# A fused linear-attention and SiLU feed-forward kernel: first states from PSUM by VectorE, weight pieces in one row, a new order of tasks

## The chip, the cores and the metric

The kernel runs on one core of one Trainium2 chip. The metric is device time in microseconds (us) of one execution of the whole program. Lower is better.

## What is computed

The reference has two parts. The first is a gated linear recurrence over 768 steps, for each of 4 batches and 8 heads with head dimension 48:

```python
f = 1.0 / (1.0 + np.exp(-f_logit))
for t in range(S):
    state = f[:, :, t, :, None] * state + einsum('bhd,bhe->bhde', k[:, :, t], v[:, :, t])
    y[:, :, t] = einsum('bhd,bhde->bhe', q[:, :, t], state)
```

The second part takes the rows `y` as a 3072 x 384 matrix `x` (batch and step as rows, head and dimension as columns) and gives `silu(x @ w_in) @ w_out`, with `w_in` 384 x 2048 and `w_out` 2048 x 384. Inputs and output are float32.

## The kernel before, in words

**Tiling.** Each batch's 768 steps are cut into 6 chunks of 128. Two chunks make a pair; there are 12 pairs P. Pairs 0 to 3 (form "T") hold chunks 0 and 1 of one batch and interleave even and odd steps, so each DMA row is 384 bytes. Pairs 4 to 11 (form "N") hold the same chunk of two batches, with rows of 192 bytes.

**The stages of a pair,** with the name that each has as a task (`P` pair, `i` one of its two chunks):

- `f`, `k`, `q`, `v`: input loads, issued on SP's queue (line 239). A whole pair's tensor is 128 x 768 float32, listed as 384 KB; `k.4.0` and `k.4.1` are halves.
- `E` (line 246) and `L` (lines 258, 261): ScalarE exp and log, which give the log of the gate. `cs` (lines 322 to 332): TensorE sums it along the steps by a triangular matrix. `ia` and `a` (line 334): ScalarE exp of plus and minus that sum. `al` (lines 276, 336): the decay over the chunk.
- `ki` and `qg` (line 339): k times `ia` and q times `a`, on VectorE (letter V) or GpSimd (G). `vb` (line 341): v cast to bf16.
- `tq` (line 346) and `qkc` (line 185 or 187, called from 350 or 352): the transposition of k and q by TensorE and its copy out of PSUM, or `qkD` (line 354): the same by a DMA on SP's queue.
- `sc` (lines 363, 367): the products of q and k. `at` (line 371): VectorE masks them, two per chunk. `y` (lines 283, 379, 383): the output rows; `yi` is the part that comes from the earlier state, where it is issued apart.
- `d` (lines 295, 400): k times v, summed over the chunk, in PSUM. `sd` (lines 404, 406) adds the earlier state, or only copies `d` into SBUF for the first chunk of a batch. `su` (line 414) multiplies by the decay into the bf16 state `st`. It is two instructions, one for each half of the head pairs, of 48 partitions and 4 x 48 elements.
- `yc`, `yT`, `xc` (lines 387, 391, 393): y to bf16, transposed by TensorE, copied; or `yD` (line 395) by a DMA on SP's queue.
- `mi` (line 269): 8 tasks a pair, x @ w_in, each for 256 of the 2048 columns; pairs 0 and 1 have each in two halves, for one chunk each (`mi.0.3.1` is pair 0, task 3, chunk 1). `si` (line 274): ScalarE SiLU. `mo` (line 304): 4 tasks a chunk, the product with w_out. `oc` (line 307), `so` (lines 314, 316): out of PSUM, and stored.
- `wi` (line 216) and `wo` (line 219): the weights in 4 pieces each, cast from float32 to bf16 by DMAs that GpSimd issues. `wi.n` serves tasks `mi` 2n and 2n+1, `wo.n` the n-th `mo` of each chunk.
- `idle`: TensorE products of zeros into a free PSUM bank (line 459), `idle.512.5::2` being 5 of 512 columns into bank 2.

**What sets the order.** The text PLAN names every task with its engine letter (A ScalarE, V VectorE, G GpSimd, S SP, P TensorE) and, after the second colon, the buffers that it takes. Tasks are issued in that order (line 504), and each engine and queue works its own in the order given. A task waits for its data and for the former users of its buffer; one that waits holds back all that stand behind it on its engine. ScalarE loads a table (line 507) at each change between exp/log and SiLU. Ahead of the plan stand masks and memsets (lines 479 to 503).

In the plan before, POOL's queue (GpSimd) has `wi` and `wo` between other tasks: `su.0.0 wi.1 ki.2.1 wi.0 qg.2.0 qg.2.1 wi.2 su.1.0 wi.3 su.0.1 vb.2.1 wo.0 su.2.0 ki.3.0 wo.1 qg.3.0 wo.2 vb.3.1 su.2.1 vb.3.0 wo.3`. SP's queue begins `f.0.0 f.0.1 f.2.0 f.1.0 q.0.0 k.0.0 k.1.0 v.0.0 q.1.0 f.3.0 k.2.0 q.2.0 v.1.0 f.4.0 v.2.0 q.3.0 k.3.0`.

Of the kernel before, what the change touches and what calls it, by code (L numbers as in the profile page):

```python
# [53 lines left out]
mi.2.2:P:4 si.2.3:A:2 si.1.7:A: tq.3.1:P:7 v.4.0:S:5 si.2.0:A: mi.2.1:P:1 qkc.3.1:V:1 si.0.6:A: mo.0.1.0:P:6 si.2.1:A: vb.3.1:G:6 tq.3.0:P:3
su.2.1:G:0 si.1.6:A: mi.2.5:P:7 qkc.3.0:V: si.1.5:A: mi.2.7:P:2 vb.3.0:G:0 si.2.5:A: wo.3:G: mo.0.0.0:P:1 si.2.7:A: v.5.0:S:0 si.2.2:A: ki.4.1:G:3
d.3:P:5,0 sd.3.0:V:0 sc.3.0:P:3,7 sc.3.1:P:2,4 su.1.1:G:0 at.3.0.1:V:2 mo.0.0.1:P: at.3.1.0:V:3 E.5.0:A:0 mo.2.1.0:P:5 su.3.0:G:0 mo.1.1.0:P:7
L.5.0:A:2 f.6.0:S:2 mo.1.1.1:P: sd.3.1:V:1 at.3.1.1:V: mo.0.0.2:P: at.3.0.0:V: mo.2.1.1:P: y.3:P:2,0 mo.1.1.2:P: q.4.1:S:4 mi.2.6:P:4 mi.2.4:P:3
# [4 lines left out]
vb.5.1:A:2 mo.2.0.3:P: qkD.4.1:S:0 mi.3.1:P:7 oc.2.0:V:3 vb.4.0:V:3 mi.3.0:P:2 si.3.2:A:3 oc.2.1:V:4 si.3.3:A: qg.4.0:V: mo.1.0.2:P: si.3.5:A:
mi.3.6:P:0 q.6.0:S: ki.5.0:G:4 si.3.1:A: f.8.0:S:3 tq.4.0:P:3 si.3.0:A: so.1.1:G: mi.3.4:P:5 vb.4.1:A:4 qg.5.0:V: q.7.0:S:1 vb.6.1:A:5 qg.5.1:V:1
mo.1.0.3:P: si.3.4:A: ki.5.1:G: cs.6.1:P:1 qkc.4.0:A:1 mi.3.7:P:4 cs.6.0:P:7 si.3.7:A: d.4.0:P:2 qkD.5.0:S:2 mo.3.1.0:P:5 sd.4.0:V:0 si.3.6:A:
oc.1.0:V:5 vb.5.0:A:0 mo.3.1.1:P: sc.4.1:P:3,4 sc.4.0:P:2,0 at.4.1.0:V:0 mo.3.1.2:P: qkD.5.1:S:3 a.6.1:A:2 at.4.0.0:V:1 mo.3.0.0:P:6 E.8.0:A:0
# [4 lines left out]
mi.4.0:P:7 si.4.7:A: si.4.1:A: tq.6.0:P:4 si.4.0:A: y.5.0:P:0 k.8.1:S:1 mi.4.6:P:2 qkc.6.0:A:1 yc.5.0:V:1 k.7.0:S:2 mi.4.5:P:1 si.4.4:A: so.0.0:S:  # L70
y.5.1:P:7 si.4.2:A: mo.4.0.0:P:0 su.5.1:G:0 si.4.5:A: v.7.0:S:2 mo.4.1.0:P:4 yc.5.1:A:2 vb.8.1:A:6 su.4.1:G:0 sc.6.1:P:3,6 si.4.6:A: sc.6.0:P:1,7
q.7.1:S: at.6.1.0:V:0 mo.4.0.1:P: yD.5.0:S:0 at.6.0.0:V:1 cs.8.1:P:2 mo.4.1.1:P: at.6.1.1:V: E.7.0:A:1 at.6.0.1:V: cs.8.0:P:3 yT.5.1:P:1 mo.4.0.2:P:
sd.5.0:V:1 L.7.0:A:2 k.8.0:S: vb.7.0:G:3 y.6.1:P:6 v.10.0:S:3 su.5.0:G:0 a.8.1:A:0 y.6.0:P:7 ia.8.0:A:2 so.3.0:S: mo.4.1.2:P: ia.8.1:A:3 mo.4.0.3:P:
# [467 lines left out]
```

## Time and profile before

| | before |
|---|---|
| median of the runs | 182.53 us (182.09, 182.53, 183.05) |
| the profiled execution | 181.74 us |
| its span, first to last instruction | 179.9 us |
| TensorE busy | 170.3 us |
| ScalarE busy | 134.9 us |
| VectorE busy | 83.2 us |
| GpSimd busy | 59.9 us |
| mean granted TensorE clock | 0.991 |

The span is what the trace covers; the profiled execution's own time is 1.84 us longer, for what lies around the instructions. A timeline row gives start, duration, engine, line, operation, and `out<-in`; in square brackets stands the idle time of the engine just before, and what ended it. A row of the chain gives start, length, and the engine and line that the chain runs through. A row by stretches gives length, then busy time and count for TensorE matmul (PE), weight load, VectorE (DVE), ScalarE (ACT) and GpSimd (POOL), then granted clock, DMA share and GB/s. A row by groups gives count, total busy us, mean ns of one, then idle before. A DMA queue's row gives packets, MB and share of the time of 16 engines; q1 carries what SP issues, q0 what GpSimd issues.

### The profile page before, as it was taken

The page shows a single profiled execution, that of the slowest core. Times are in us where ns is not written, and L with a number is a line of the kernel's source. Part 1 is how long each engine was busy: PE and PEld are TensorE (multiplying, and loading weights), DVE is VectorE, ACT ScalarE, POOL GpSimd, SP SyncE. Part 2 cuts the span into 40 slices and gives each one's busy share as a digit, 9 for nine tenths or more (in the row PEclk, how much of TensorE's full clock was granted, in tenths as well). Part 3 has the DMA queues.
Part 4 walks back from the last instruction along what each step waited for, and adds up shares of the span by engine and source line. Part 5 has one row for each costly group of instructions (what it writes and reads, how often), then busy time and mean ns, then how long its engine had stood idle before and what let it go on. Part 6 is the DMA issues. An engine that isn't in the chain of part 4 may idle for free.

```text
span 179.9 us, 4982 instructions
## 1 busy us (share of the span) xinstructions
PE 170.3 (95%) x2039; PEld 130.0 (72%) x2040; DVE 83.2 (46%) x165; ACT 134.9 (75%) x252; POOL 59.9 (33%) x107
## 2 busy tenths in 40 slices
...
GB/s 142 315 321 309 202 242 256 230 209 193 180 176 182 203 201 134 210 204 207 158 106 221 178 202 205 125 218 170 216 156 122 213 127 26 109 26 131 0 154 112
DMA packets 109574, 31.91 MB, mean 177 GB/s; under 512 B 103536, under 2 KB 109088, under 8 KB 109552
## 3 DMA queue, kind: packets, MB, share of 16 engines
...
q8 instruction: 16, 0.26, 0.6%
...
HBM read 25.17 MB, written 4.72 MB: 166 GB/s over the span
## 4 chain that ended last, share of the span: by engine, by line
PE 84%; ACT 6%; DVE 3%; DMA 2%; issue 2%; POOL 0%; POOLq 0%; DVEq 0%
PE pb L304 33%; PE pb L269 33%; PE pb L459 3%; DMA xT<-yb 2%; ACT x L334 2%; PE pb L346 2%; PE pb L379 2%; PE pb L383 2%; PE pb L367 2%; DVE atm L371 2%; PE pb L329 2%; DVE qk L339 1%; PE pb L391 1%; PE pb L295 1%; PE pb L363 1%
## 5 line engine op out<-in xcount | busy, mean ns | idle before, releaser
L304 PE MATMUL pb<-w_out_sb,hT 128*128 128x384 bf16 (+1 forms) x416 | 70.7, 313 | 0.1
L269 PE MATMUL pb<-xT,w_in_sb 128*128 128x256 bf16 (+1 forms) x672 | 70.1, 257 | 0.7 <-DMA xT<-yb 0.5
L274 ACT ACTIVATE hT<-pb 128x512 bf16<-128x512 f32 x96 | 51.0, 611 | 23.2 <-PE pb L269 23.1
L269 PEld LDWEIGHTS <-w_in_sb 128*128 128x128 bf16 x672 | 56.9, 98 | 8.2 <-issue 0.9
L304 PEld LDWEIGHTS <-hT 128*128 128x128 bf16 x416 | 37.9, 97 | 18.1
L414 POOL TENSOR_TENSOR st<-sd,al 48x192 bf16<-48x192 f32 x40 | 20.6, 516 | 54.7 <-PE pb L379 18.2
L371 DVE TENSOR_TENSOR atm<-pb,triu 128x512 bf16<-128x512 f32 x32 | 20.0, 682 | 15.2 <-PE pb L367 15.2
L187 DVE COPY ob<-pb 128x384 f32<-128x384 f32 (+1 forms) x16 | 8.3, 526 | 36.0 <-PE pb L304 35.9
L334 ACT ACTIVATE x<-pb 128x384 f32<-128x384 f32 x48 | 22.0, 511 | 3.3 <-PE pb L329 1.5
L507 ACT ACT_TABLE_LOAD x17 | 21.8, 1283 | 0.3
L339 POOL TENSOR_TENSOR qk<-k,x 128x384 bf16<-128x384 f32 x11 | 11.4, 1038 | 14.9 <-DVE vb L187 13.5
L339 DVE TENSOR_TENSOR qk<-k,x 128x384 bf16<-128x384 f32 x13 | 11.9, 936 | 8.3 <-DMA k<-in_k_dram 5.4
L404 DVE TENSOR_TENSOR sd<-pb,st 128x384 f32<-128x384 f32 x16 | 8.6, 550 | 12.6 <-PE pb L400 6.1
L316 POOL DMA_DIRECT2D out_dram<-ob x7 | 4.0, 569 | 29.5 <-ACT ob L185 21.1
L339 DVE TENSOR_TENSOR qk<-q,x 128x384 bf16<-128x384 f32 x17 | 11.4, 688 | 3.3 <-DMA q<-in_q_dram 1.8
L246 ACT ACTIVATE e<-f 128x768 f32<-128x768 f32 (+1 forms) x13 | 10.5, 804 | 2.0 <-DMA f<-in_f_logit_dram 2.0
L185 ACT CAST yb<-pb 128x384 bf16<-128x384 f32 x16 | 7.6, 490 | 3.6 <-PE pb L383 2.4
L371 DVE TENSOR_TENSOR atm<-pb,mask 128x512 bf16<-128x512 f32 x16 | 10.1, 680 | 0.4 <-PE pb L363 0.4
L339 POOL TENSOR_TENSOR qk<-q,x 128x384 bf16<-128x384 f32 x7 | 7.1, 1019 | 7.4 <-ACT x L334 5.8
L459 PE MATMUL pb<-zero,triu 128*128 128x512 bf16 x19 | 7.1, 525 | 1.5 <-POOL triu masks.py:66 1.4
L185 ACT COPY ob<-pb 128x384 f32<-128x384 f32 (+1 forms) x10 | 4.4, 456 | 4.6 <-PE pb L304 4.6
L346 PE MATMUL pb<-ident,qk 128*128 128x128 bf16 x80 | 6.7, 234 | 0.4 <-DVE atm L371 0.4
...
## 6 DMA issues: line engine op xcount, KB each, us to landing
f<-in_f_logit_dram SPq DMA_DIRECT2D x11, 384.0 KB, 5.5
...
q<-in_q_dram SPq DMA_DIRECT2D x4, 384.0 KB, 5.2
k<-in_k_dram SPq DMA_DIRECT2D x4, 384.0 KB, 4.9
v<-in_v_dram SPq DMA_DIRECT2D x4, 384.0 KB, 7.3
w_in_sb<-in_moe_w_in_dram POOLq DMA_DIRECT2D x4, 384.0 KB, 7.5
```

Source lines behind the costliest of these rows:

```text
L185: nc.scalar.copy(dst, src)
L246: return nc.scalar.activation(e, at("f", P)[:, j * w:(j + 1) * w], AF.Exp, scale=-1.0)
L269: nc.tensor.matmul(h[:, i, cols], w_in_sb[:, kk, n * 128:(n + 1) * 128], at("xT", P)[:, kk, cols], start=(kk == 0), stop=(kk == KT - 1))
L274: return nc.scalar.activation(at("hT", P)[:, 2 * j:2 * j + 2, :], at("h", P, j).rearrange("p (n c) -> p n c", n=2), AF.Silu)
L304: nc.tensor.matmul(at("o", P, i)[:, cols], at("hT", P)[:, n, i * C:(i + 1) * C], w_out_sb[:, n, cols], start=(n == 0), stop=(n == NT - 1))
L334: nc.scalar.activation(at(kind, P, i).rearrange("p h d -> p (h d)"), at("cs", P, i)[:, 0:HD], AF.Exp, scale=1.0 if kind == "ia" else -1.0)
L339: ENG[eng].tensor_mul(at("qk", P, i)[:, j, :, 0:D], heads("qk"[j], P, i), at("ia" if j else "a", P, i))
L346: nc.tensor.transpose(t_ps[:, j, p, :], at("qk", P, i)[:, j, 2 * p:2 * p + 2, :], ident)
L371: ENG[eng].tensor_mul(at("atm", P, i)[:, r], at(f"s{r}", P, i).rearrange("p (n c) -> p n c", c=C), mask[:, None, :].to_broadcast([C, NP, C]))
L414: ENG[eng].tensor_mul(at("st", P, i)[lo:lo + D, :, r * D:(r + 1) * D], src[lo:lo + D, :, r * D:(r + 1) * D], al_of(P, i)[lo:lo + D, :, Non ...
L459: nc.tensor.matmul(buf["pb", int(got)][:, 0:rest[0]], triu, zero[:, 0:rest[0]], start=True, stop=True, skip_group_check=True)
L507: nc.scalar.preload_act_table_set(TABLES[mode])
```

## The change

Three things change.

1. `sd.0.0`, `sd.1.0`, `sd.2.0` (ScalarE) and `sd.3.0` (VectorE), the copies of a first chunk's `d` out of PSUM, are no longer in the plan. `su.0.0`, `su.1.0`, `su.2.0` and `su.3.0` move from GpSimd to VectorE and read `d` from PSUM (line 411).
2. POOL's queue begins `vb.1.1 ki.1.0 qg.1.1 wi.1 wi.2 wi.0 ki.2.0 qg.2.0 qg.2.1 wi.3 wo.0 wo.1 su.0.1 wo.2 wo.3 ki.3.0 su.1.1 ki.3.1`: all eight weight pieces stand behind the tasks of the pairs 0 and 1.
3. The whole PLAN is new: order, buffers, and the engine of some tasks (`oc` on ScalarE 10 to 15, `xc` 4 to 8, `yc` 16 to 12; `qg` on GpSimd 7 to 11; `so` on POOL's queue 12 to 15). The other tasks are the same, 10 `tq`, 14 `qkD`, 12 `yT` and 12 `yD` among them. The `idle` products are 24 instead of 20, all ahead of the first `mi`.

Two further edits in the code do nothing with this plan: the pair's halves are of one chunk, so `b, c` come out as before, and no pair of form T has a `qkD`.

```diff
-f.0.0:S:0 f.0.1:S: f.2.0:S:1 f.1.0:S:2 q.0.0:S:0 E.0.0:A:0 E.0.1:A: k.0.0:S:0 L.0.0:A:0 L.0.1:A: idle.512.11::0 cs.0.1:P:0 E.2.0:A:1 k.1.0:S:1
...
-idle.512.3::3 sc.0.0:P:3,7 al.2:A:1 ia.2.0:A:4 su.0.0:G:0 sc.0.1:P:5,1 f.4.0:S:0 at.0.0.1:V:0 E.3.0:A:0 at.0.0.0:V: tq.1.0:P:7 al.1:A:2 a.2.0:A:2
-wi.1:G: v.2.0:S:2 at.0.1.0:V:1 tq.1.1:P:2 L.3.0:A:0 qkc.1.1:V:1 qkc.1.0:A: ki.2.1:G:4 idle.512.1::3 cs.3.1:P:3 at.0.1.1:V: cs.3.0:P:4 a.3.1:A:1
-ki.2.0:V:0 wi.0:G: sc.1.0:P:5,2 ia.3.1:A:0 at.1.0.0:V:2 y.0:P:7,1 a.2.1:A:3 qg.2.0:G: al.3:A:3 yc.0.0:A:0 at.1.0.1:V: q.3.0:S:3 sc.1.1:P:6,3
-vb.1.1:A:2 yi.0.1:P: qg.2.1:G: at.1.1.1:V:3 yT.0.0:P:5 vb.1.0:A:3 tq.2.0:P:7 yc.0.1:A:1 at.1.1.0:V: d.1:P:2,3 a.3.0:A:4 wi.2:G: yT.0.1:P:1 sd.1.0:A:1
-tq.2.1:P:6 xc.0.1:V:0 ia.3.0:A:2 xc.0.0:V: su.1.0:G:0 k.3.0:S:3 y.1:P:2,1 qkc.2.0:A:0 sd.0.1:V:0 mi.0.3.0:P:4 yc.1.0:V:2 mi.0.3.1:P: wi.3:G:
...
+f.2.0:S:0 k.0.0:S:0 f.0.1:S:1 f.0.0:S: E.2.0:A:0 f.1.0:S:2 L.2.0:A:0 v.1.0:S:0 q.0.0:S:0 idle.512.11::0 cs.2.1:P:0 E.0.1:A:1 E.0.0:A: k.1.0:S:1
+cs.2.0:P:1 L.0.1:A:1 L.0.0:A: E.1.0:A:0 q.1.0:S:1 idle.512.1::2 cs.0.0:P:2 cs.0.1:P:3 a.0.0:A:0 vb.1.1:G:0 f.3.0:S:3 L.1.0:A:2 ia.0.1:A:1 cs.1.0:P:4
+a.0.1:A:2 qg.0.0:V:0 v.0.0:S:1 cs.1.1:P:5 ia.1.0:A:3 ki.0.1:V:1 al.1:A:0 ia.0.0:A:4 qg.0.1:V: al.0:A:1 ia.1.1:A:0 k.2.0:S:2 ki.0.0:V: vb.1.0:A:1
+idle.512.4::6 tq.0.1:P:6 ki.1.0:G:2 ia.2.0:A:1 tq.0.0:P:7 qkc.0.1:V:0 a.1.0:A:2 q.2.0:S:2 qkc.0.0:A: qg.1.0:V: ki.1.1:V:3 a.1.1:A:4 idle.512.3::2
+tq.1.0:P:2 q.3.0:S:3 a.2.0:A:3 qg.1.1:G: sc.0.0:P:3,4 qkc.1.0:A:1 sc.0.1:P:6,7 at.0.0.1:V:0 k.3.0:S:3 wi.1:G: at.0.0.0:V: E.3.0:A:1 idle.512.2::5
+tq.1.1:P:5 at.0.1.0:V:1 wi.2:G: d.1:P:1,4 qkc.1.1:A: v.2.0:S:2 su.1.0:V:0 wi.0:G: at.0.1.1:V: al.2:A:2 L.3.0:A:0 idle.512.3::2 sc.1.0:P:2,3 ki.2.0:G:4
+sc.1.1:P:6,1 at.1.0.1:V:2 vb.0.0:A:2 cs.3.1:P:5 vb.0.1:A:3 at.1.1.0:V:3 qg.2.0:G: al.3:A:3 ia.2.1:A:2 d.0:P:7,3 at.1.1.1:V: a.2.1:A:0 cs.3.0:P:6
+ia.3.1:A:4 su.0.0:V:0 qg.2.1:G:2 y.0:P:0,1 a.3.0:A:1 at.1.0.0:V: yc.0.0:A:0 yi.0.1:P: tq.2.0:P:7 a.3.1:A:3 wi.3:G: yc.0.1:V:1 ia.3.0:A:0 y.1:P:0,2
+wo.0:G: ki.2.1:V: yc.1.0:A:2 yT.0.0:P:5 sd.0.1:V:0 yi.1.1:P: yT.0.1:P:1 yc.1.1:A:0 tq.2.1:P:6 xc.0.0:V:0 wo.1:G: xc.0.1:A: qkc.2.0:V:0 v.3.0:S:3
+yT.1.0:P:0 yT.1.1:P:3 xc.1.0:A:1 mi.0.2.0:P:2 qkc.2.1:V: su.0.1:G:0 xc.1.1:A: mi.0.3.0:P:5 mi.1.3.0:P:1 sd.1.1:V:1 mi.1.3.1:P: qg.3.0:V:3 wo.2:G:
+mi.0.2.1:P: sc.2.1:P:7,0 si.1.3:A:0 wo.3:G: qg.3.1:V:0 sc.2.0:P:3,6 at.2.1.1:V:0 mi.1.5.1:P:4 mi.1.2.1:P:1 at.2.0.0:V:1 mi.1.2.0:P: at.2.0.1:V:
+mi.0.3.1:P: mi.1.4.1:P:0 at.2.1.0:V: mi.1.4.0:P: mi.0.5.0:P:3 si.1.4:A: mi.1.0.0:P:6 mi.1.1.1:P:7 mi.1.0.1:P: f.5.0:S:0 mi.1.5.0:P: si.1.0:A:
+mi.0.1.1:P:0 si.0.3:A:1 mi.0.1.0:P: mi.0.5.1:P: si.1.5:A: ki.3.0:G: mi.0.0.0:P:6 si.0.1:A: mi.0.6.0:P:5 mi.0.0.1:P: su.1.1:G:0 mi.0.7.1:P:4 si.0.0:A:
+mi.0.7.0:P: si.0.2:A: mi.0.6.1:P: ki.3.1:G: mi.1.1.0:P: si.0.6:A: mi.1.7.0:P:0 tq.3.0:P:6 mi.1.7.1:P: qkc.3.0:A:1 mi.0.4.0:P:2 tq.3.1:P:5 si.1.7:A:
+mi.0.4.1:P: f.4.0:S:1 mo.0.0.0:P:6 qkc.3.1:A: mo.0.1.0:P:0 si.1.1:A: mi.1.6.1:P:5 si.0.5:A: mi.1.6.0:P: si.1.2:A: mo.1.1.0:P:7 si.1.6:A: mo.0.1.1:P:
...
+mo.3.0.0:P:7 si.3.2:A: q.7.0:S:1 oc.2.1:A:5 at.4.1.1:V: cs.6.1:P:5 mo.3.0.1:P: si.3.6:A: y.4.1:P:2 d.5.1:P:0 v.6.0:S:2 yc.4.1:V:0 su.4.1:G:0
...
@@ -234,6 +234,8 @@
                 n = 2 // parts
                 w = n * HD
+                if n == 1:
+                    b, c = us[j][0] - j, us[j][1]
@@ -351,7 +353,11 @@
         elif kind == "qkD":
-            nc.sync.dma_start_transpose(out=at("qkT", P, i).rearrange("p j n c -> p (j n) c"), in_=at("qk", P, i).rearrange("p j h d -> p (j h d)"))
+            if T:
+                dst = at("qkT", P).rearrange("p j n g s c -> p (j n) g s c")[:, :, :, i]
+            else:
+                dst = at("qkT", P, i).rearrange("p j n c -> p (j n) c")
+            nc.sync.dma_start_transpose(out=dst, in_=at("qk", P, i).rearrange("p j h d -> p (j h d)"))
```

More of the change, by code (lines that the diff above doesn't have):

```diff
@@ L54 @@
[L54 to L57, printed above, removed]
@@ L62 @@
[L62 to L65, printed above, removed]
@@ L70 @@
[L70 to L73, printed above, removed]
@@ new lines @@
+mi.2.0:P:6 xc.3.1:V: su.2.1:G:0 mi.3.6:P:3 si.2.3:A:2 mi.3.1:P:4 qg.4.0:V: si.2.7:A: k.4.1:S: su.3.1:G:0 si.2.5:A: mi.3.7:P:5 si.3.1:A:3 f.6.0:S:2
+mi.2.6:P:7 vb.5.1:A:0 si.3.7:A: d.4.0:P:0 v.4.1:S: mi.2.1:P:4 sd.4.0:V:0 si.2.6:A: qg.4.1:V:2 tq.4.0:P:5 si.2.4:A: mi.3.2:P:0 si.2.1:A: k.7.0:S:1
+si.2.0:A: mi.3.0:P:7 ki.4.1:G: qkc.4.0:A:0 cs.5.1:P:1 mi.3.5:P:4 qkD.4.1:S:1 si.3.0:A: mo.2.1.0:P:6 si.2.2:A: si.3.5:A: sc.4.0:P:5,7 v.7.0:S:1
+at.4.0.1:V:0 mo.2.1.1:P: k.5.0:S: at.4.0.0:V: mi.3.4:P:2 q.6.0:S:0 cs.5.0:P:4 ia.5.1:A:4 mo.2.1.2:P: al.5.1:A:1 al.5.0:A:0 ia.5.0:A:1 ki.5.1:V:4
@@ new lines @@
+mo.2.0.0:P:7 E.6.0:A:0 vb.4.1:V:1 f.7.0:S:3 mo.2.0.1:P: vb.5.0:A:2 v.9.1:S:3 a.5.1:A:2 mo.2.0.2:P: L.6.0:A:0 qg.5.1:G: d.4.1:P:5 mo.2.0.3:P:
+sd.4.1:V:1 a.5.0:A:3 y.4.0:P:1 mi.3.3:P:5 yc.4.0:V:2 su.4.0:G:0 oc.2.0:V:4 mo.2.1.3:P: si.3.3:A: f.8.0:S:1 si.3.4:A: sc.4.1:P:4,1 at.4.1.0:V:1
+mo.3.0.0:P:7 si.3.2:A: q.7.0:S:1 oc.2.1:A:5 at.4.1.1:V: cs.6.1:P:5 mo.3.0.1:P: si.3.6:A: y.4.1:P:2 d.5.1:P:0 v.6.0:S:2 yc.4.1:V:0 su.4.1:G:0
+mo.3.0.2:P: ia.6.1:A:0 cs.6.0:P:4 k.6.0:S: yT.4.0:P:6 E.7.0:A:1 ki.5.0:V:0 so.2.0:G: mo.3.0.3:P: qg.5.0:V: qkD.5.1:S:2 mo.3.1.0:P:1 L.7.0:A:1
@@ new lines @@
+si.4.3:A: sc.5.0:P:3,1 k.8.0:S:2 ki.6.0:V: si.4.2:A: mo.4.1.0:P:6 at.5.0.0:V:3 si.4.5:A: q.7.1:S: yT.5.1:P:0 mo.4.0.0:P:7 at.5.0.1:V: mo.4.1.1:P:
+qg.6.1:V: al.7.1:A:5 y.5.0:P:2 qkD.6.1:S:0 a.7.1:A:0 cs.8.1:P:5 yc.5.0:A:2 tq.6.0:P:3 ia.7.1:A:3 d.6.0:P:1 qkc.6.0:V:1 vb.7.1:A:3 cs.8.0:P:2
+yD.5.0:S:1 mo.4.0.1:P: ia.8.0:A:1 ki.7.1:V:4 ia.8.1:A:2 sc.6.0:P:4,3 qg.7.1:V: al.8.0:A:1 a.8.0:A:4 mo.4.0.2:P: qkD.7.0:S:2 a.8.1:A:3 at.6.0.1:V:0
+xc.5.1:A: mo.4.1.2:P: qg.8.1:G:0 at.6.0.0:V: qkD.7.1:S:3 d.6.1:P:2 sd.6.0:V:1 mo.4.0.3:P: su.5.0:G:0 mo.4.1.3:P: d.7.0:P:3 oc.4.1:A:4 sd.6.1:V:0
@@ new lines @@
+mi.7.1:P:7 si.7.4:A: oc.5.1:A:0 y.8.1:P:3 k.9.1:S: si.7.6:A: mi.7.5:P:5 so.5.1:G: yc.8.1:V:1 si.7.1:A: vb.9.1:V:5 v.10.1:S:4 mi.7.0:P:4 su.6.0:G:0
+si.7.5:A: cs.9.1:P:2 si.7.0:A: sc.8.0:P:6,3 q.11.0:S:5 at.8.0.1:V:1 mi.7.7:P:7 at.8.0.0:V: mo.7.0.0:P:5 k.10.1:S: si.7.7:A: si.7.2:A: mo.7.1.0:P:4
+so.3.0:S: cs.9.0:P:3 y.8.0:P:6 mo.6.0.0:P:7 yD.8.1:S:0 a.9.1:A:0 mo.7.0.1:P: yc.8.0:A:2 qg.9.1:G:1 ia.9.1:A:3 mo.7.1.1:P: ia.9.0:A:1 yD.8.0:S:
+E.10.0:A:0 ki.9.1:G: mo.7.0.2:P: mo.7.0.3:P: al.9.0:A:4 a.9.0:A:2 ki.9.0:G:2 qkD.9.1:S:3 L.10.0:A:1 mo.6.0.1:P: qg.9.0:V: mo.6.1.1:P: qkD.9.0:S:2
@@ new lines @@
+mo.8.1.0:P:6 sd.9.0:V:1 yc.9.1:A:1 yD.9.0:S:1 a.10.1:A:3 d.9.1:P:3 E.11.0:A:1 mo.8.0.0:P:2 qg.10.1:G: yD.9.1:S: mo.8.1.1:P: L.11.0:A:2 su.9.0:G:0
+mo.8.0.1:P: a.10.0:A:1 qkD.10.1:S:1 cs.11.0:P:4 oc.6.0:A:0 mo.8.0.2:P: a.11.0:A:2 ia.11.0:A:4 cs.11.1:P:5 qg.11.0:V:3 mo.8.1.2:P: a.11.1:A:0
+sd.9.1:V:1 ia.11.1:A:3 mo.8.1.3:P: vb.11.1:V:3 qg.10.0:V: mi.9.4:P:0 ki.11.0:V: qkD.10.0:S:0 mi.9.0:P:7 vb.10.1:V:4 si.9.4:A:0 vb.10.0:V:1 mi.9.3:P:4
+ki.11.1:G:2 qkD.11.0:S:2 mi.9.6:P:3 si.9.3:A: qg.11.1:G: mi.9.2:P:5 si.9.6:A: si.9.0:A: mi.9.1:P:0 so.6.0:G: qkD.11.1:S:3 si.9.2:A: su.9.1:G:0
```

83 lines of the change are left out of this document (33 added, 50 removed).

## The prediction

> **What bounds the kernel now.** I read the page first, then the span cut at the first and behind the last product with the weights, then the chain of waits about the cut.
>
> ```profile
> span 179.9 us, 4982 instructions
> PE 170.3 (95%) x2039; PEld 130.0 (72%) x2040; DVE 83.2 (46%) x165; ACT 134.9 (75%) x252; POOL 59.9 (33%) x107
> PE 84%; ACT 6%; DVE 3%; DMA 2%; issue 2%; POOL 0%; POOLq 0%; DVEq 0%
> ```
>
> ```profile
> 0.00:25.17 25.17, 19.50 (x285) 12.33 (x287) 17.43 (x47) 19.55 (x41) 11.04 (x29) 0.93 1.06 259
> 25.17:176.77 151.60, 150.78 (x1760) 117.64 (x1754) 65.73 (x119) 115.09 (x212) 48.90 (x79) 1.00 0.84 166
> 176.77:179.90 3.13, 0.00 (x0) 0.00 (x0) 0.00 (x0) 0.31 (x1) 0.00 (x0) 1.00 0.26 84
> ```
>
> TensorE bounds it. Behind 25.17, where the first `mi` starts, it stands still for only 151.60 - 150.78 = 0.82 us until its last product. What another order can win there is under 1 us. The last 3.13 us are one copy and the last stores, the same in both orders. So the question is when the first `mi` starts, and whether the new order keeps the rest as full. What held that start?
>
> ```profile
> 17.94 1.69 DVE qk L339
> 19.63 1.18 issue
> 20.80 0.69 DVE atm L371
> ...
> 21.53 0.48 PE pb L391 x3
> ```
>
> ```profile
> 18.48 1.97 POOL L339 TENSOR_TENSOR qk<-q,x 128x384 bf16<-128x384 f32 x2
> 17.86 3.02 DVE L339 TENSOR_TENSOR qk<-k,x 128x384 bf16<-128x384 f32 x1
> 138.35 0.99 POOL L339 TENSOR_TENSOR qk<-q,x 128x384 bf16<-128x384 f32 x1
> 138.41 1.35 DVE L339 TENSOR_TENSOR qk<-k,x 128x384 bf16<-128x384 f32 x1
> ```
>
> ```profile
> 20.00:21.00 1.00, 0.00 (x0) 0.00 (x0) 1.00 (x2) 0.75 (x3) 1.00 (x2) 1.00 1.24 181
> 21.00:22.00 1.00, 0.47 (x5) 0.47 (x5) 1.00 (x2) 0.40 (x1) 0.17 (x1) 0.50 1.16 184
> 23.00:24.00 1.00, 1.00 (x21) 0.86 (x17) 0.27 (x1) 0.35 (x1) 0.00 (x0) 0.50 1.09 266
> 25.00:26.00 1.00, 1.00 (x36) 0.96 (x28) 0.90 (x3) 0.43 (x1) 1.00 (x2) 1.00 1.20 212
> ```
>
> `ki.2.0` on VectorE lasts 3.02 us, until 0.43 behind the two `qg` of GpSimd (20.45). The later pair of rows repeats it: GpSimd ends at 139.34, VectorE at 139.76. So a product of two SBUF operands on VectorE that meets one on GpSimd ends 0.42 behind it. Behind `ki.2.0` stand four `at`; TensorE's `yT.0.0` needs their bank, and TensorE does nothing from 20 or just before to 21.53. Then its clock is granted at 0.50 up to about 24.6: 3 us at half speed, 1.5 of them lost. In all the old start loses about 3 us here.
>
> **The change, part by part.** *First states.*
>
> ```profile
> L185 ACT COPY sd<-pb 128x384 f32<-128x384 f32 x3 | 1.5, 512 | 2.2 <-PE pb L295 2.2
> L414 POOL TENSOR_TENSOR st<-sd,al 48x192 bf16<-48x192 f32 x40 | 20.6, 516 | 54.7 <-PE pb L379 18.2 <-DVE sd L404 10.9 <-DVE qk L339 9.1
> L187 DVE COPY ob<-pb 128x192 f32<-128x192 f32 x2 | 0.7, 358 | 21.4 <-PE pb L304 21.4
> L187 DVE COPY sd<-pb 128x384 f32<-128x384 f32 x1 | 0.6, 557 | 1.8 <-ACT hT L274 1.8
> L497 DVE MEMSET st<- 128x192 uint32 x4 | 0.8, 218 | 0.0
> ```
>
> Removed: 3 x 0.512 on ScalarE, 0.557 on VectorE, 8 x 0.516 = 4.1 on GpSimd. Added: 8 VectorE products of 192 elements from PSUM. No row shows one; the bounds are 0.218 (192 elements written, none read) and 0.557 (384 from PSUM). I take 0.36, the row of 192 from PSUM: 2.9 us in all. On TensorE's path this is worth nothing: the chain above runs through no `sd` or `su`. In the new order `su.0.0` lies just ahead of `yi.0.1`; at 0.557 it costs up to 0.4. I take 0: VectorE is otherwise ahead of ScalarE there.
>
> *Loads.* Units of 0.393 MB:
>
> ```profile
> q1 hardware_dynamic: 2129, 0.80, 62.1%
> q1 hardware_dynamic: 4192, 1.58, 115.1%
> 5.85 0.84 ACT L246 ACTIVATE e<-f 128x768 f32<-128x768 f32 x1 [0.35 <-DMA f<-in_f_logit_dram]
> ```
>
> The queue's rows are 0 to 5 us and 5 to 10 us: 0.316 MB/us from 5 on. The first two units (0.79) were moved by 5.0, and the exp on the second (`f.2`), which waited for the load, started at 5.85: 0.85 from moved to usable. In the new order `f.0` is the third unit (1.18 MB): 5 + 0.38/0.316 + 0.85 = 7.05; before it was the first. `f.1` is usable at 8.3, `k.1` (seventh) at 12.0. That is the price of putting `f.2` and `k.0` ahead.
>
> *The start.* In the new order ScalarE sets it.
>
> ```profile
> 4.58 0.92 ACT L258 ACTIVATE lf<-e 128x384 bf16<-128x384 f32 x2
> 8.98 1.58 ACT L258 ACTIVATE lf<-e 128x768 bf16<-128x768 f32 x2
> 10.50 2.03 ACT L334 ACTIVATE x<-pb 128x384 f32<-128x384 f32 x5
> 13.13 1.09 ACT L185 COPY qkTT<-pb 128x1024 bf16<-128x1024 bf16 x1
> 19.32 0.96 ACT L185 CAST vb<-v 128x384 bf16<-128x384 f32 x2
> ```
>
> Ends overlap the next start by about 0.1 to 0.2, so the steps are 0.41, 0.75, 0.39, 0.89 and 0.42. From 7.05: `E.0.0` and two halves of `L` to 8.3, `E.1.0` to 9.05. Then, up to `yc.1.1`, which frees the bank of `mi.0.2.0`: 3 whole E or L (2.25), 16 `ia` or `a` (6.24), 4 `al` (0.4, an estimate), 3 `qkc` (2.67), 3 `vb` (1.26), 3 `yc` (1.2): 14.0, which is 23.05. One wait lies inside: `ki.1.0` on GpSimd starts at 12.25 (`k.1` at 12.0, behind a product of VectorE), ends at 13.25, so `ki.0.0` on VectorE ends at 13.7, `tq.0.0` at 14.2; ScalarE has come to `qkc.0.0` at 13.55. That adds 0.65: 23.7. Beside it `vb.0.1` ends at about 20.2, `d.0` takes 0.45, then VectorE's `su.0.0` 0.7 and `at.1.0.0` 0.6: 22.0; its `yc.0.1`, `ki.2.1`, `sd.0.1` (0.55, 0.55, 0.5) and `xc.0.0` (0.35) end at 23.9. With 0.1 or so at each of the last handovers I take the first `mi` at **24.4**; 23.9 would be none of them. `ki.2.0` and both `qg` of pair 2 are on GpSimd now, with `at` and `su` from PSUM on VectorE beside them, so the stall of 3.02 us has no place.
>
> What TensorE has done by then differs by three small tasks:
>
> ```profile
> 26.01 0.17 PE pb L379 x4
> 26.52 0.17 PE pb L391 x3
> ```
>
> `yi.1.1` and both `yT` of pair 1 lie ahead of the first `mi` now: 3 x 0.17 = 0.51 less behind it. The other work is the same; the four extra `idle` lie in gaps of the start.
>
> *The sum.* (24.4 - 25.17) - 0.51 = -1.28 us, with the rest as full as before. 181.74 - 1.28 = 180.46 for the profiled execution. Its own time lies 0.79 under the median, so 182.53 - 1.28 = **181.25**, rounded 181.2.
>
> *Weights.*
>
> ```profile
> w_in_sb<-in_moe_w_in_dram POOLq DMA_DIRECT2D x1, 384.0 KB, 6.8
> q0 software_dynamic: 704, 0.70, 110.6%
> q1 hardware_dynamic: 299, 0.08, 9.9%
> q1 hardware_dynamic: 14366, 5.08, 100.5%
> q1 hardware_dynamic: 307, 0.12, 31.9%
> q1 hardware_dynamic: 505, 0.13, 29.2%
> ```
>
> The second and third rows are the stretch 19 to 23, with two pieces in the queue; then come 0 to 19, 25 to 27 and 29 to 31. Back to back, weights move at 0.175 MB/us: 2.25 us a piece. `wi.1` is issued at about 16.6 behind `qg.1.1` and lands at 23.4, then one each 2.25: `wi.2` 25.7, `wi.0` 27.9, `wi.3` 30.2, `wo.0` 32.4, `wo.3` 39.2. TensorE asks for them at 24.4, 26.7, 29.0, 31.7, 35.9 and 41.7 (24.4 plus the work in between, 0.33 for half a `mi`, 0.65 for a `mo`). All are 1 to 3 us early, so I cost them at nothing; each us of lateness would be paid in full.
>
> **The rivals.** *1. The inputs starve behind the weights (slower).* In 19 to 23 the weights took everything: SP's loads moved 0.08 MB, 0.02 a us. Now the weights run without a gap from 19 to about 37. `k.3` is the fourteenth unit (5.51 MB); 5.08 were moved by 19, 0.43 are left. `ki.3.0`, `su.1.1`, `ki.3.1` follow it on GpSimd (1.0, 1.1, 1.0), and TensorE wants `tq.3.0` at 34.0 and `tq.3.1` at 35.2. It decides from a landing at 32 on. At 0.02 a us `k.3` lands at 38 and TensorE loses 6 us. For it: that row. Against: over 25 to 27 and 29 to 31, beside a single piece, the loads kept 0.06 a us, which lands `k.3` at 27. [...] In the middle, a landing at 34 or 35, it costs 3 us: **184.2**; at its worst 187.
>
> *2. Given back at the joints (no change).* From the start of `sc.4.1` to `y.4.1` the new order has 1.84 us of TensorE work, and about 2.2 to 2.4 at 5.0, 9.0 and 10.1; the old had one such place (1.85), else 3 or more. Two `at` of 0.68 and a `sc` of 0.28 fill 1.64 with no wait. Each 0.3 us late, at four places, gives 1.2 us back: **182.5**. For it: VectorE has `oc` and `yc` ahead of those `at`. Against: the old order too was this tight once and lost 0.82 in all.
>
> *3. The start stalls again (slower).* If the descriptor writing of `wi.3`, `wo.0`, `wo.1` holds `ki.2.1` as GpSimd's products do (the 3.02 us began beside such an issue), it ends 1.6 late, TensorE stands idle and its clock halves, 1.5 more: 181.2 + 3.1 = **184.3**. Against: GpSimd's work there is no tensor operation. [...]
>
> **How the numbers follow.** Forecast 0.46; rival 1 0.20; rival 2 0.22; rival 3 0.12. A measurement of this kernel tells about 0.5% (0.9 us) from no change. The forecast lies beyond it (faster 0.46), rival 2 within (same 0.22), rivals 1 and 3 slower (0.32). The forecast's own range is 180.0 (start at 23.6) to 181.6. The range goes to 179.6 below and through the middle of rivals 1 and 3 to 185.4; it leaves out the worst of rival 1 and a little below, 0.15.
>
> **What would show it.** Right: the first `mi` at 23.9 to 24.9; no TensorE gap over 1.3 us and clock 1.00 from 15 to 26; no `sd` copy; `su` from PSUM at 0.3 to 0.4 each on VectorE. Rival 1: TensorE waiting at `tq.3` (line 346) about 34, GpSimd's `ki.3.0` waiting for the DMA of k. Rival 2: several waits of line 379 or 383 for `at`. Rival 3: 0.50 in the clock near 22 to 26. The prediction is wrong if TensorE's idle time behind the first `mi` exceeds 2 us, or that start comes after 25.5.

## The result, and the profile after

The new kernel takes **181.64 us** (median of 14 runs, 180.93 to 182.22) beside 182.52 of the kernel before (181.93 to 184.05): a ratio of 0.9947, 95% interval 0.9922 to 0.9971. Two later measurements put the same pair further apart: 181.71 beside 184.04 (0.9878, 0.983 to 0.9926) and 181.68 beside 184.03 (0.9871, 0.9839 to 0.9903). The new kernel's own time hardly changes, that of the kernel before does; so each experiment is set below beside the kernel before as it was measured together with it. Medians are of all executions, while the ratios and their intervals leave out the slow ones (over 1.5% above the fastest of the same kernel), so a ratio can differ a little from that of the medians.

The page after, its span, its busy times and its chain:

```profile
span 179.2 us, 4981 instructions
PE 170.5 (95%) x2042; PEld 129.0 (72%) x2044; DVE 79.7 (44%) x166; ACT 132.7 (74%) x251; POOL 61.6 (34%) x106
PE 77%; ACT 9%; DVE 4%; DMA 3%; SPq 2%; issue 1%; POOL 1%; DVEq 0%
```

The same span cut at the first product with the weights and behind the last one (columns as before):

```profile
0.00:23.58 23.58, 19.12 (x299) 11.73 (x301) 15.72 (x49) 19.97 (x41) 13.02 (x30) 1.00 1.07 271
23.58:176.17 152.59, 151.40 (x1747) 117.31 (x1744) 63.98 (x118) 112.44 (x210) 48.55 (x76) 1.00 0.84 165
176.17:179.20 3.03, 0.01 (x1) 0.00 (x0) 0.00 (x0) 0.32 (x1) 0.00 (x0) 1.00 0.38 130
```

These three rows and their counterparts of before give the whole account of the two profiled executions (180.93 us after, 181.74 before):

| | before | after | change |
|---|---|---|---|
| first `mi` starts | 25.17 | 23.58 | -1.59 |
| TensorE idle behind it | 0.82 | 1.19 | +0.37 |
| TensorE busy behind it | 150.78 | 151.40 | +0.62 |
| behind its last product | 3.13 | 3.03 | -0.10 |
| span | 179.9 | 179.2 | -0.7 |

The start won 1.59 us and the dense part gave back 0.99. The rows of the start (the line numbers have moved by 2 to 6):

```profile
5.83 1.18 ACT L248 ACTIVATE e<-f 128x384 f32<-128x384 f32 x2
11.44 1.06 POOL L341 TENSOR_TENSOR qk<-k,x 128x384 bf16<-128x384 f32 x1 [2.04 <-ACT al L278]
11.56 1.36 DVE L341 TENSOR_TENSOR qk<-k,x 128x384 bf16<-128x384 f32 x1
13.41 1.01 ACT L185 COPY qkTT<-pb 128x1024 bf16<-128x1024 bf16 x1 [0.48 <-PE pb L348]
17.12 0.72 DVE L420 TENSOR_TENSOR st<-pb,al 48x192 bf16<-48x192 f32 x2 [0.17 <-PE pb L297]
15.83 2.46 POOL L216 DMA_DIRECT2D w_in_sb<-in_moe_w_in_dram  x3
23.58 1.84 PE L271 MATMUL pb<-xT,w_in_sb 128*128 128x128 bf16 x30
```

The exp of pair 0 starts at 5.83; VectorE's product that meets GpSimd's ends at 12.92, 0.42 behind it (12.50); a first state from PSUM costs 0.36. The clock was granted at 1.00 throughout. And there is one new thing, in the scores of pair 2:

```profile
25.35 0.52 PE L369 MATMUL pb<-qkTT 48*64 48x128 bf16 x21
26.72 0.36 PE L369 MATMUL pb<-qkTT 48*64 48x128 bf16 x11 [0.85 <-issue]
```

In the middle of one `sc`, with nothing to wait for that the profile shows, TensorE stands still for 0.85 us.

### The profile page after: what moved, and what is told of

Its sections match the earlier page's. It is cut to its first block, busy times and chain, and to the rows that moved or that the text cites. A ratio compares the mean times of both kernels' runs of the same rounds, so it can differ in the third digit from the quotient of the medians.

```text
span 179.2 us, 4981 instructions
## 1 busy us (share of the span) xinstructions
PE 170.5 (95%) x2042; PEld 129.0 (72%) x2044; DVE 79.7 (44%) x166; ACT 132.7 (74%) x251; POOL 61.6 (34%) x106
## 3 DMA queue, kind: packets, MB, share of 16 engines
HBM read 25.17 MB, written 4.72 MB: 167 GB/s over the span
## 4 chain that ended last, share of the span: by engine, by line
PE 77%; ACT 9%; DVE 4%; DMA 3%; SPq 2%; issue 1%; POOL 1%; DVEq 0%
PE pb L306 32%; PE pb L271 32%; ACT hT L276 4%; DMA q<-in_q_dram 3%; PE pb L373 2%; SPq L241 2%; PE pb L385 2%; PE pb L348 2%; PE pb L389 2%; DVE qk L341 2%; ACT L513 1%; DVE atm L377 1%; PE pb L331 1%; PE pb L397 1%; DVE st L420 1%
## 5 line engine op out<-in xcount | busy, mean ns | idle before, releaser
L271 PE MATMUL pb<-xT,w_in_sb 128*128 128x256 bf16 (+1 forms) x672 | 68.9, 257 | 0.0
L420 POOL TENSOR_TENSOR st<-sd,al 48x192 bf16<-48x192 f32 x32 | 16.6, 518 | 18.7 <-PE pb L385 12.1
L341 POOL TENSOR_TENSOR qk<-q,x 128x384 bf16<-128x384 f32 x11 | 11.3, 1025 | 31.9 <-ACT x L336 14.5
L185 ACT COPY ob<-pb 128x384 f32<-128x384 f32 (+1 forms) x15 | 6.8, 453 | 12.6 <-PE pb L306 12.6
L187 DVE COPY ob<-pb 128x384 f32<-128x384 f32 (+1 forms) x11 | 5.8, 535 | 22.2 <-PE pb L306 22.2
L318 POOL DMA_DIRECT2D out_dram<-ob x8 | 4.6, 578 | 28.4 <-ACT ob L185 24.8
L316 POOL DMA_DIRECT2D out_dram<-ob x14 | 7.6, 548 | 19.6 <-DVE ob L187 15.9
L341 DVE TENSOR_TENSOR qk<-q,x 128x384 bf16<-128x384 f32 x13 | 7.6, 593 | 13.7 <-ACT x L336 13.7
L185 ACT CAST yb<-pb 128x384 bf16<-128x384 f32 x12 | 5.6, 479 | 9.7 <-PE pb L389 9.6
L341 DVE TENSOR_TENSOR qk<-k,x 128x384 bf16<-128x384 f32 x14 | 9.9, 710 | 0.9 <-ACT x L336 0.9
L187 DVE CAST yb<-pb 128x384 bf16<-128x384 f32 x12 | 6.6, 556 | 8.0 <-PE pb L389 5.9
```

The lines of the kernel that those rows point to most:

```text
L185: nc.scalar.copy(dst, src)
L187: ENG[eng].tensor_copy(dst, src)
L271: nc.tensor.matmul(h[:, i, cols], w_in_sb[:, kk, n * 128:(n + 1) * 128], at("xT", P)[:, kk, cols], start=(kk == 0), stop=(kk == KT - 1))
L341: ENG[eng].tensor_mul(at("qk", P, i)[:, j, :, 0:D], heads("qk"[j], P, i), at("ia" if j else "a", P, i))
L420: ENG[eng].tensor_mul(at("st", P, i)[lo:lo + D, :, r * D:(r + 1) * D], src[lo:lo + D, :, r * D:(r + 1) * D], al_of(P, i)[lo:lo + D, :, Non ...
```

## The experiments

Each edit is to PLAN alone. Theory A is that of the prediction: the old start lost by the held `ki.2.0` and the slow clock behind it, and the first states are worth nothing by themselves. Its rival stands beside it in the texts on record. The first four were measured together, beside a time before of 184.06 us.

### 1. One part alone: the first states

The kernel before, with `su.0.0` in the place of `sd.0.0`, and pairs 1 to 3 alike:

```diff
-sd.0.0:A:0
+su.0.0:V:0
...
-su.0.0:G:0
```

> The order before, with only the first part of the change: the four copies sd of the first chunks are gone, su.0.0 to su.3.0 are on VectorE from PSUM, in the place where the copies stood. Theory A (the start was held by ki.2.0 on VectorE and by the clock, and the first states lie off the path): no change, 182.0 to 183.0, first mi at 25.0 to 25.4, su at 0.36 each. Theory B (the first states bring the gain of the new kernel): 181.2 to 181.9, first mi at 24.4 or earlier.

184.88 us, 1.0095 (1.0049 to 1.014): slower, and neither theory had expected that. Three views say why: GpSimd's and ScalarE's timeline, TensorE's, and the DMA queues from 14 to 16 us.

```profile
10.26 0.95 POOL L216 DMA_DIRECT2D w_in_sb<-in_moe_w_in_dram  x1
17.91 0.84 ACT L246 ACTIVATE e<-f 128x768 f32<-128x768 f32 x1 [3.09 <-DMA f<-in_f_logit_dram]
18.86 0.61 PE L346 MATMUL pb<-ident,qk 128*128 128x128 bf16 x8 [2.07 <-ACT al L276]
27.46 0.84 PE L269 MATMUL pb<-xT,w_in_sb 128*128 128x128 bf16 x12
```

```profile
q0 software_dynamic: 269, 0.27, 83.5%
q1 hardware_dynamic: 303, 0.12, 32.4%
```

In the kernel before, `wi.1` stood behind `su.0.0` on GpSimd and was issued at 15.71. With `su.0.0` gone it is issued at 10.26, in the midst of the loads. From 14 to 16 us these move 0.12 MB; in the same stretch of the kernel before:

```profile
q1 hardware_dynamic: 1701, 0.64, 116.0%
```

So `f.3` comes 3 us late, ScalarE waits 3.09 for it, `al` waits behind it, TensorE waits 2.07 for the bank that `al` frees, and from 20.2 the clock is granted at 0.50. The first `mi` starts at 27.46, 2.29 later than in the kernel before.

### 2. The stall of the old start alone: `ki.2.0`

The kernel before, with one task moved:

```diff
-ki.2.0:V:0 wi.0:G:
+wi.0:G:
...
-qg.2.0:G:
+qg.2.0:G:0 ki.2.0:G:
```

> The order before, with one task moved: ki.2.0 from VectorE to GpSimd, between qg.2.0 and qg.2.1. Theory A: the four at end by about 20.2, TensorE's gap about 20 falls below 1 us, the clock stays at 1.00, the first mi comes at 23.0 to 24.0, the time falls by 1.2 to 2.2 us to 180.3 to 181.3. Rival (the loads, the weights or ScalarE would hold the start at 25 anyway): first mi at 24.8 to 25.4, 182.0 to 183.0.

181.95 us, 0.9884 (0.9814 to 0.9953): 2.1 us less than the 184.06 beside it. That is the fall that theory A named; its 180.3 to 181.3 had been reckoned from 182.5. TensorE's first product with the weights:

```profile
23.19 0.84 PE L269 MATMUL pb<-xT,w_in_sb 128*128 128x128 bf16 x12 [0.55 <-ACT qkTT L185]
```

It starts at 23.19 in place of 25.17, with the clock at 1.00. One product moved from VectorE to GpSimd gives what the whole change gives, as far as can be told.

### 3. The other part undone: copies and GpSimd back in the new order

The new kernel, and pairs 1 to 3 alike, with `sd.3.0` on VectorE as it was:

```diff
-su.0.0:V:0
+sd.0.0:A:0 su.0.0:G:0
```

> The new kernel with the copies of the first chunks back (three on ScalarE, one on VectorE) and su.0.0 to su.3.0 on GpSimd. Theory A: the new kernel's time within 0.4, 181.3 to 182.0; the copies cost ScalarE 1.1 ahead of the first mi, which moves by 0.4 to 0.9. Theory B: the gain is gone, 182.3 or more, first mi at 24.7 or later.

185.29 us, 1.0074 (1.0035 to 1.0114), some 2% over the new kernel by the ratios. The first `mi` comes at 27.64. Theory A's numbers fail here and theory B's hold. TensorE's waits, then its timeline, then two stretches:

```profile
PE pb L385 <- POOL st L420: 2.9, 2, 1.9
```

```profile
23.67 0.33 PE L385 MATMUL pb<-st,qkTT 128*128 128x96 bf16 x4 [1.90 <-POOL st L420]
```

```profile
23.00:24.00 1.00, 0.33 (x6) 0.33 (x6) 0.00 (x0) 0.09 (x1) 0.85 (x3) 0.93 1.21 205
24.00:25.00 1.00, 1.00 (x20) 0.80 (x20) 0.97 (x2) 0.28 (x1) 1.00 (x2) 0.50 1.17 195
```

`su.0.0` on GpSimd now stands behind the weights' issues and pair 2's products; `yi.0.1` waits 1.90 us for it, and right behind this wait the clock is granted at 0.50. Three of the twelve executions kept a mean clock of 1.00; they took 183.7 to 183.8 us, so the wait costs time without the slow clock too. The new order needs its first states on VectorE.

### 4. The wait on issue: more instructions

Theory F: TensorE's own instructions are brought in blocks by a DMA queue of their own (`q8 instruction` on the new kernel's page: 16 packets of together 0.26 MB, 16 KB each), and the block came late behind the weights. To move the boundary of a block and nothing else, the 24 `idle` of 512 columns become 96 of 128, the other five groups like this one:

```diff
-idle.512.11::0
+idle.128.44::0
```

> The new kernel with each product of zeros of 512 columns replaced by four of 128: the same TensorE time, 72 products and 72 weight loads more ahead of the first mi. Theory F (the 0.85 us in the midst of sc.2.0 near 25.9 is TensorE's own instructions arriving late; they come in blocks of 16 KB by a queue of their own): the stall leaves that place; it is gone, or stands some 144 instructions earlier in the work; if gone, 180.5 to 181.2. Rival (sc.2.0 waits for data or for a bank): the stall stays in sc.2.0, 181.3 to 182.0.

183.57 us, 0.9977 (0.9931 to 1.0023), about 1% over the new kernel by the ratios. The wait has left the scores, as theory F has it, and has grown, which neither theory had. TensorE's timeline; what was done before the wait (products, then weight loads, in the first two counts); and the q8 row of 23.2 to 23.3 us:

```profile
25.51 0.46 PE L385 MATMUL pb<-st,qkTT 128*128 128x96 bf16 x4 [2.71 <-issue]
```

```profile
0.00:25.00 25.00, 18.54 (x351) 15.37 (x352) 16.11 (x49) 19.26 (x39) 14.19 (x33) 1.00 1.02 248
```

```profile
q8 instruction: 1, 0.02, 59.2%
```

The same two views of the new kernel, the second for 24.4 to 24.5 us:

```profile
0.00:26.40 26.40, 21.41 (x349) 13.75 (x352) 18.54 (x54) 22.76 (x45) 15.69 (x35) 1.00 1.08 264
```

```profile
q8 instruction: 1, 0.02, 60.4%
```

Whatever task stands there, the wait comes behind the 352nd weight load (the products differ by the few records that a trace lacks). And TensorE goes on some 2.3 us behind the start of the block's packet both times: 25.51 behind 23.2, 26.72 behind 24.4. Behind the wait the clock is granted at 0.50 until 29.0. The profiled execution took 184.51 us. Five of the twelve kept a mean clock of 0.998 or more, with a median of 182.56; in those the wait was probably shorter.

### 5. The same, with still more instructions, most of them ahead of 6 us

The boundary is met some 100 products and 100 weight loads earlier. By theory F the block should then be there in time; this was the author's estimate, as no run shows when a block is asked for. The new kernel, with the other five groups as in experiment 4:

```diff
-idle.512.11::0
+idle.64.72::0
```

The next four were measured together, beside a time before of 184.04 us.

> The new kernel with more and narrower idle products: 72 of 64 columns in place of the first 11 of 512, and 4 of 128 for each other one of 512; some 200 TensorE instructions (products and weight loads counted) more, all but 78 of them before 6 us. Nothing but the idle products changes. [...] Theory G (the wait on issue of 0.85 us comes from the place, the switch between products and scores, and not from a block): it stays at about 0.85 in the scores of pair 2, and the time is that of the new kernel within 0.3 us.

183.2 us, 0.9981 (0.9948 to 1.0014). The wait at about 26 us is gone, as theory F has it, and theory G falls. But the time, which by theory F should fall by about the wait, is 1.5 us more than the new kernel's 181.71 beside it: the next boundary brings a wait of 0.63 of its own at 29.25, with its packet at 27.0 beside the weights, and the first `mi` is 1.4 us later (24.97).

```profile
29.25 1.95 PE L271 MATMUL pb<-xT,w_in_sb 128*128 128x128 bf16 x32 [0.63 <-issue]
```

```profile
0.00:29.00 29.00, 22.76 (x479) 19.29 (x480) 19.74 (x56) 22.88 (x45) 17.00 (x36) 1.00 1.05 250
```

```profile
11.54 0.56 DVE L341 TENSOR_TENSOR qk<-q,x 128x384 bf16<-128x384 f32 x1 [7.32 <-DMA q<-in_q_dram]
```

480 weight loads are 128 more than 352, and with 128 products they make 256 instructions: one block. The last row is `qg.0.0`, which waits for a load until 11.54 (10.14 in the new kernel). The first exp, which waits for its load too, is 0.35 late (4.40 in place of 4.05); what delays the loads was not tried by itself and stays open.

### 6. The row of weights undone

The new kernel, with `wi.2` and `wi.0` behind `qg.2.1`:

```diff
-at.0.1.0:V:1 wi.2:G: d.1:P:1,4
+at.0.1.0:V:1 d.1:P:1,4
...
-wi.0:G: at.0.1.1:V:
+at.0.1.1:V:
...
-qg.2.1:G:2
+qg.2.1:G:2 wi.2:G: wi.0:G:
```

> The new kernel with the weight pieces wi.2 and wi.0 issued behind qg.2.0 and qg.2.1 on GpSimd in place of ahead of ki.2.0; the other pieces as before. [...] Rival (the row of weights is needed where it is): wi.2 lands after 27, TensorE waits for it in the products of pair 1, and the time is 0.5 to 1.5 us more than the new kernel's.

182.81 us, 0.9942 (0.9912 to 0.9973), 0.6% over the new kernel's 181.71 beside it. TensorE's timeline, and its waits:

```profile
26.38 0.36 PE L369 MATMUL pb<-qkTT 48*64 48x128 bf16 x11 [0.16 <-issue]
27.54 0.68 PE L271 MATMUL pb<-xT,w_in_sb 128*128 128x128 bf16 x9 [0.79 <-DMA w_in_sb<-in_moe_w_in_dram]
```

```profile
PE pb L271 <- DMA w_in_sb<-in_moe_w_in_dram: 1.4, 3, 0.8
PE pb L306 <- DMA w_out_sb<-in_moe_w_out_dram: 0.4, 1, 0.4
```

The wait on issue falls to 0.16, as theory F lets one expect, but 1.8 us of waits for weights come in its place: on the time the rival was right. Beside the new kernel of experiment 7 (0.68) the wait is 0.52 shorter: TensorE goes on 0.34 earlier (26.38 in place of 26.72), with the block's packet at 24.0 in place of 24.4, and reaches the boundary 0.18 later. So the row costs some 0.3 us of late instructions and saves 1.8.

### 7 and 8. The new kernel and `ki.2.0` alone, on one chip

> The new kernel unchanged, beside the others on one chip. Both theories: 0.995 of the time before, first product with the weights at 23.6, the wait on issue of 0.8 to 0.9 us at about 26.5.

> The kernel before with ki.2.0 alone moved to GpSimd between qg.2.0 and qg.2.1, again, beside the new kernel on one chip. If its lead on the new kernel (0.988 beside 0.995 of the time before, from two chips) is real: 0.987 to 0.991, and 0.5 to 1.3 us under the new kernel. If it was the noise of the other chip: 0.993 to 0.997, the same as the new kernel within 0.4 us.

181.71 us, 0.9878 (0.983 to 0.9926), first `mi` at 23.75, wait on issue 0.68; and 182.31 us, 0.9925 (0.989 to 0.996), first `mi` at 23.04. In experiment 2 `ki.2.0` alone had 0.9884. Side by side its lead is gone, and it is 0.6 us behind; the intervals overlap, so which of the two is faster can't be told.

### 9, 10 and 11. Two attempts at a better version

The kernel of experiment 2, with two products and their `si` exchanged:

```diff
-mi.7.4:P:7
+mi.8.5:P:7
...
-si.7.4:A:
+si.8.5:A:
...
-mi.8.5:P:7
+mi.7.4:P:7
...
-si.8.5:A:
+si.7.4:A:
```

> The kernel before with ki.2.0 on GpSimd between qg.2.0 and qg.2.1, and in addition the products mi.7.4 and mi.8.5 (and their si) changed for each other. In that kernel without the exchange TensorE waited 0.82 us at 122.07 for the transposition by DMA that mi.7.4 reads; the exchange lets one product of about 0.7 us go first. If that wait is a true loss: it falls below 0.2 us, and the time to 0.984 to 0.990 of before, under both kernels. If another wait takes its place (the products of pair 8 are then used up before the rest of pair 7 is there): the sum of TensorE's waits stays, 0.988 to 0.993.

The new kernel, with two products ahead of the scores:

```diff
-mi.0.2.1:P: sc.2.1:P:7,0
+mi.0.2.1:P: mi.0.3.1:P: mi.1.5.1:P:4 sc.2.1:P:7,0
```

> The new kernel with mi.0.3.1 and mi.1.5.1 ahead of sc.2.1 and sc.2.0, so that the block boundary of TensorE's instructions is met some 0.3 us later (a product with the weights is longer than a score, so fewer instructions pass in a us). Theory F: the block is usable at 26.6 to 26.8 us wherever the boundary lies, so the wait on issue falls from 0.68 to 0.85 us to 0.3 to 0.5 and TensorE gains 0.3 us, 0.998 of the new kernel. Theory G (the place, between products and scores): the wait stays at 0.7 to 0.9. If wi.2 lands after 25.6 a wait of mi.1.5.1 takes the gain.

> The new kernel once more, beside the two on one chip. 0.988 to 0.995 of the time before; wait on issue 0.7 to 0.9 us near 26.5.

Beside a time before of 184.03: 181.98 us (0.9889, 0.9857 to 0.992), 181.55 (0.9867, 0.9838 to 0.9896) and 181.68 (0.9871, 0.9839 to 0.9903). Neither attempt can be told from the new kernel beside it. In the first the wait for the transposition is gone, but two late blocks cost 1.01 us ahead of 27.20 and 0.81 ahead of 33.67. In the second the wait on issue falls to 0.45, within what theory F had:

```profile
27.54 0.53 PE L369 MATMUL pb<-qkTT 48*64 48x128 bf16 x23 [0.45 <-issue]
```

But theory F had the block usable at 26.6 to 26.8 wherever the boundary lies, and TensorE went on at 27.54: the block's packet itself came later, at 25.1 in place of 24.4. Why it did stays open. The 0.13 us between the medians are below what can be told.

All the waits on issue together, each with the tenth of a us in which its q8 packet began:

| kernel | products, weight loads before it | packet | goes on | wait |
|---|---|---|---|---|
| after | 349, 352 | 24.4 | 26.72 | 0.85 |
| 4 | 351, 352 | 23.2 | 25.51 | 2.71 |
| 5 | 479, 480 | 27.0 | 29.25 | 0.63 |
| 6 | 349, 352 | 24.0 | 26.38 | 0.16 |
| 7 | 349, 352 | 24.4 | 26.72 | 0.68 |
| 9 | 349, 351 | 24.9 | 27.20 | 1.01 |
| 9, second | 477, 479 | 31.3 | 33.67 | 0.81 |
| 10 | 349, 352 | 25.1 | 27.54 | 0.45 |
| 11 | 349, 352 | 24.4 | 26.71 | 0.71 |
| 12 | 350, 351 | 23.8 | 26.17 | 0.70 |

The count is the same each time, or one block further, and it is always 2.2 to 2.4 us from packet to product.

### 12. The first states again, with the gate kept

The kernel of experiment 1, with `wi.1` behind `ki.2.1`:

```diff
-wi.1:G: v.2.0:S:2
+v.2.0:S:2
...
-ki.2.1:G:4
+ki.2.1:G:4 wi.1:G:
```

> The kernel before with the first states on VectorE from PSUM, as in the first experiment, but with the issue of wi.1 put behind ki.2.1 on GpSimd, so that it goes out at about 16 to 17 us as in the kernel before, and not at 10.3. Theory H (the loss of the first experiment is that of the weights: with su.0.0 gone from GpSimd nothing held wi.1 back, it took the DMA engines from 13.3 to 17, and f.3 came 3 us late): the exp of f.3 starts at 14.5 to 15.2 again, TensorE's wait of 2.1 us for al goes, the first product with the weights starts at 24.8 to 25.6, and the time is that of the kernel before, 0.997 to 1.003. Theory V (VectorE is late with at and so TensorE waits): f.3 in time, but the first product with the weights still at 26.5 or later, 1.006 to 1.012.

182.6 us beside 183.13, 0.9959 (0.9914 to 1.0003). ScalarE, VectorE, GpSimd and TensorE:

```profile
14.61 0.84 ACT L246 ACTIVATE e<-f 128x768 f32<-128x768 f32 x1
18.29 0.55 DVE L339 TENSOR_TENSOR qk<-k,x 128x384 bf16<-128x384 f32 x1
18.61 2.03 POOL L339 TENSOR_TENSOR qk<-q,x 128x384 bf16<-128x384 f32 x2
22.89 0.84 PE L269 MATMUL pb<-xT,w_in_sb 128*128 128x128 bf16 x12
124.43 5.84 PE L269 MATMUL pb<-xT,w_in_sb 128*128 128x256 bf16 x52 [1.16 <-DMA xT<-yb]
```

Theory H holds: `f.3` is in time (14.61), the wait for `al` is gone, and so is the loss of experiment 1. Theory V falls. What neither had: the first `mi` starts at 22.89, earlier than in any other kernel here, because `ki.2.0` on VectorE, started at 18.29 and so 0.32 ahead of GpSimd's products, took 0.55 us in place of 3.02. Part of that is given back, 1.16 us at 124.43 (0.47 in the kernel before) and 0.70 on issue.

## Why the prediction was right, and where it was not

**What held the old start: right, and shown, though its size was smaller.** Experiments 2 and 8 take away the held `ki.2.0` alone and have the first `mi` at 23.19 and 23.04, in the profiled executions with a full clock. That is 2.0 to 2.1 us of the 3 or so that the prediction put down to it.

**The first states: the price right, "worth nothing" not.** They cost 0.36 each, as taken. But the step looked only at the old path of TensorE. It did not ask, for the task that left GpSimd, what stood behind it there: the issue of `wi.1`, which `su.0.0` held back until 15.71. Alone the part costs 0.9%; with the gate kept, nothing that can be told (0.9914 to 1.0003). In the new order `qg.1.1` is the gate and the weights are issued at 15.83, so the two parts of the change belong together, and taking the first one out costs some 2% (experiment 3).

**Loads and start: the loads priced too high, and ScalarE not alone.** `f.0` was taken to be usable at 7.05; the exp started at 5.83. The load is in two halves, `f.0.1` ahead of `f.0.0`, and the exp on the first needs 0.98 MB and not 1.18; the working counted both, which is 0.6 us. The rest is that the queue had moved 0.88 MB by 5.0 in place of 0.80, and that 0.85 from moved to usable was too much: this exp did not wait for its load at all. Against that, both halves of the exp and of the log took 1.90 us, from 5.83 to 7.73, where the working had counted 1.25 for one exp and two logs. The wait ahead of `qkc.0.0` was 0.48 (0.65 predicted). So the first `mi` came at 23.58 in place of 24.4, outside the bounds of 23.9 to 24.9.

The prediction also had ScalarE set the start, with VectorE ahead of it and the first states at 0. The chain that ends at the first `mi` says otherwise; some of its pieces:

```profile
5.24 4.81 DMA q<-in_q_dram
10.62 2.31 DVE qk L341 x3
13.41 1.01 ACT qkTT L185
14.42 0.40 ACT x L336
17.87 2.48 DVE atm L377 x4
20.36 0.26 DVE st L420
20.63 0.37 DVE st L420
```

From 10 us to the first `mi` it leads through ScalarE for 1.41 us only, and for longer through VectorE, the two first states `su.1.0` and `su.0.0` among its tasks. The sum of ScalarE's work came out close all the same, because ScalarE too was nearly full: it stood idle for 0.63 us from 10 to 23.

**Weights at nothing: right, and the row is why.** In the new kernel none of TensorE's waits is for a weight; with two pieces issued later such waits cost 1.8 us (experiment 6). What the step had no term for is TensorE's own instructions, whose packets the page lists beside the loads and the weights (q8 beside q1 and q0): waits of 0.68 to 0.85 us.

**The sum: near in total by luck, as two errors cancel.** The start won 0.82 more than predicted; "the rest as full as before" failed by 0.37 of idle time, for which the wait on issue of 0.85 alone would do, and by 0.62 us more of busy time where 0.51 less was predicted. The latter was not found in any one place. The chain leads through ScalarE for 9% of the span in place of 6%, from 56 to 71 us above all; matmul ends are modelled, so a busy TensorE there may be one that is fed slowly. That stays open. And how near the total is depends on the measurement: the fall was 0.88 us in the first and 2.3 in the two later ones, where the kernel before was slower, against the 1.28 predicted.

**Rival 1** did not decide here, but loads that starve behind weights are real: in experiment 1 they moved 0.12 MB in place of 0.64 from 14 to 16 us, which cost 0.9%. The prediction's argument for it was a row of 4 us, at 0.02 MB/us for the loads; over a longer stretch they keep more. The queues of the new kernel from 26 to 39 us, then from 20 to 22:

```profile
q0 software_dynamic: 2300, 1.82, 87.8%
q1 hardware_dynamic: 2299, 0.71, 35.6%
```

```profile
q0 software_dynamic: 391, 0.39, 117.4%
q1 hardware_dynamic: 62, 0.02, 5.1%
```

From 26 to 39 the two moved as many packets, 2299 and 2300, and the loads 0.055 MB/us; from 20 to 22, early in the weights' row, they moved 62 beside 391, 0.01 MB/us. The prediction's row of 299 beside 704 mixed two such stretches: its part from 20 to 22 has 37 beside 365. **Rival 2** is half true: the dense part gave 0.99 back, though not at the named waits for `at`. **Rival 3** did not occur: `ki.2.1` took its usual 0.55 at 22.09. Its price, though, is real: behind stops of 1.90 to 2.71 us the clock was granted at 0.50 (the profiled executions of experiments 1, 3 and 4).
